# Fused attention and two MoE layers: identity products in TensorE's early gaps, an earlier rank for converting w3 and w_out, and other homes for three operands at the turn to the last product

## The chip, the cores and the metric

One Trainium2 chip, one of its cores. The metric is the device time of one execution in microseconds (us), the median over several executions.

## The reference, cut to what matters

Inputs: q, k, v of 4 batches x 8 heads x 576 positions x 64; 2304 tokens in all; weights w1, w2 (512x1024), w3 (1024x1024), w_out (1024x512), w_in (512x2048), and a second w_out (2048x512).

```python
scores = where(mask, q @ k.T / 8 - slope[h] * (i - j), -1e9)   # causal, window of 128
x = softmax(scores) @ v                                        # 2304 x 512
h = (x @ w1) * (x @ w2) @ w3 ; x = h @ w_out                   # first MoE
out = relu(x @ w_in) ** 2 @ w2_out                             # second MoE
```

The weights arrive as 64-bit floats and are turned into 32-bit floats on the chip.

## The kernel before, in words

The kernel is written as some thousands of small tasks with a rank, an engine or a choice of engines, a cost, dependencies, and the tile slots that they take and give back. A list scheduler in Python (`Plan.run`) keeps a due time for every engine and orders the tasks: among the tasks that could start within 0.1 of the earliest, the one with the lowest rank goes first. Its result is the fixed order of instructions on each engine; on the chip every engine runs its own queue in that order and waits on semaphores. So a rank does not set when something happens, only what stands ahead of it.

Five stages follow each other. **Heads** (0 to about 168 us): 16 pairs of heads. For one pair TensorE makes scores `s` from `qk` (line 437), VectorE adds the bias and takes the row minimum (line 405, `e<-s`), ScalarE takes the exponent (line 413), VectorE scales by the reciprocal sum (line 252), TensorE transposes through `ident` into the one buffer `t` (line 473, `tr0` to `tr3`), ScalarE copies it out (line 196, `pt`), and TensorE multiplies by v (lines 497 and 513). `qk`, `v` and `e` have two buffers each, `s` three. In the gaps of this stage TensorE multiplies w3 by w_out (line 613, `ww`: 8 groups of 8 products of 512 columns), so that h never has to be formed. Each 1024-column piece of w3 and w_out is loaded (1 MB), and converted by one pass on ScalarE (line 320, `cg`) and two on VectorE (lines 329 and 335, `cs` and `cn`); rank of the j-th conversion `c0 + cj*j`, rank of its load `w0 + w34*j`. Heads of pair m have ranks from `-40 + 7m`; lower goes first. All loads and stores stand in one queue, SyncE's.

The planner also puts products of `ident` by itself into gaps of TensorE (`p_warm`, line 531; results are not used): in gaps of more than 1.0 in its own account, before 40 in its own account, as many as fit, if one of the buffers `t` or `g` is free there.

Then **a, b** (lines 929 to 931), **y** and **r** (lines 1125 to 1127, 24 rounds), and last **o**, the product with the second w_out, in nine blocks of 256 tokens. All of them use a seven-product scheme (P1 to P7 on sums of quarter matrices, with operands split into a high and a low part: `oh`/`ol` for the tokens, `wh`/`wl` for the weights). At the turn from r to o the tiles of the tag `xA` (8 slots) hold the four token operands of block 0 (`lfA11` ... `lfA22` load them), the halves of the weight pieces `sm`, `ss` (`mbo5` ... `mbo7` load them, line 702; `cb` on line 716 combines them; `wlao7` and `wlbo7`, line 199, make the last low parts), and the split operand of P1. That of P2 lies in `u` (11 slots). P1 and P2 of block 0 are each cut into chunks 0 to 5 (`Q1o0`, `Q2o0`), which don't need the eighth weight piece, and chunks 6 and 7 (`P1o0`, `P2o0`), which do. The order of these products on TensorE is written out:

```python
turn = ["Q1o0", "P1o0", "Q2o0", "P2o0", "P4o0", "P6o0", "P7o0", "P5o0"]
```

The pools of the r stage (`q1`) are closed and those of the o stage (`q2`, with `fq` and `ww`) opened on their ground after r's last product.

Of the kernel before, what the change touches and what calls it, by code (L numbers as in the profile page):

```python
# [12 lines left out]
ALU = mybir.AluOpType  # L13


RANK = dict(w34=3, vv=20, w0=-15, c0=0, cj=3, h0=-40, hs=7, w12=60, wa=7, wl=9, wb=0, x0=20, mg=4, mgs=1.6, wo=1126, gg=-3, yq=1142)
B, H, S, D = 4, 8, 576, 64
NT = B * S
DM = H * D
# [11 lines left out]
class Plan:  # L31
# [7 lines left out]
    LOOK = 0.1  # L39
    SWITCH = 0.11  # L40
    STAY = 60
    FILL = 40.0

    bias = dict(d=1.0, D=0.2, a=0.3, p=0.0)

# [5 lines left out]
    def hold(self, name, tag, users):  # L51
        self.holds[name] = [tag, users]
# [6 lines left out]
    def run(self):  # L59
        tasks = self.tasks  # L60
        need = {n: len(t[3]) for n, t in tasks.items()}
        users = {}
        for n, t in tasks.items():
            for d in t[3]:
                users.setdefault(d, []).append(n)

        pool = {tag: [0.0] * c for tag, c in self.caps.items()}
        left = {h: v[1] for h, v in self.holds.items()}
        last = {h: 0.0 for h in self.holds}
        free = {}  # L70
        lock = 0.0
        end, on = {}, {}
        ready = {n for n, c in need.items() if c == 0}
        order = []
        shape = lambda n: 1 if n[:3] == "pvl" else {"qk": 1, "pv": 2}.get(n[:2], 0)
        now = 0
        while ready:
            cands = []
            for n in ready:
                rank, where, fn, deps, takes, gives, keep = tasks[n]  # L80
                t0 = 0.0
                ok = True
                for tag in {self.holds[h][0] for h in takes}:
                    p = sorted(pool[tag])
                    want = sum(self.holds[h][0] == tag for h in takes)
                    if len(p) < want + keep:
                        ok = False
                        break
                    t0 = max(t0, p[want - 1])
                if not ok:  # L90
                    continue
                best = None
                for q, w in where.items():
                    e = q.lower()
                    if e == "pe" and shape(n) != now:
                        w += self.SWITCH
                    elif e == "pe" and now:
                        rank -= self.STAY
                    t = max(t0, free.get(e, 0.0))
                    if q in "Dp":  # L100
                        t = max(t, lock)
                    for d in deps:
                        t = max(t, end[d] + (0.0 if on[d] == e else self.lat[on[d]]))
                    key = t + w + self.bias.get(q, 0.0)
                    if best is None or (key, t) < best[:2]:
                        best = (key, t, q, w)
                cands.append((best[1], rank, n, best[2], best[3]))
            assert cands, (sorted(ready)[:20], {h: (v[0], left[h]) for h, v in self.holds.items() if left[h] > 0 and any(h in tasks[n][4] for n in end)})
            t0 = min(c[0] for c in cands)
            near = [c for c in cands if c[0] <= t0 + self.LOOK]  # L110
            t, rank, n, q, w = min(near, key=lambda c: (c[1], c[0], c[2]))
            e = q.lower()
            _, _, fn, deps, takes, gives, _ = tasks[n]
            if e == "pe":
                now = shape(n)
                idle = t - free.get(e, t)
                if 1.0 < idle and t < self.FILL:
                    for tag in "tg":
                        p = pool[tag]
                        if p and min(p) <= free[e]:  # L120
                            p.remove(min(p))
                            k = f"fill{len(order)}"
                            tasks[k] = (0, {}, lambda e, tag=tag, idle=idle: self.filler(tag, int((idle - 0.4) / 0.24)), (), (), (), 0)
                            order.append((k, e, free[e], t - 0.4))
                            p.append(t)
                            break
            ready.remove(n)
            for h in takes:
                p = pool[self.holds[h][0]]
                p.remove(min(p))  # L130
            fin = t + w
            end[n], on[n] = fin, e
            free[e] = fin
            if q in "Dp":
                lock = fin
            for h in gives:
                left[h] -= 1
                last[h] = max(last[h], fin + (self.lat[e] + 0.5 if e == "dma" else 0.0))
                if left[h] == 0:
                    pool[self.holds[h][0]].append(last[h] + 0.1)  # L140
            order.append((n, e, t, fin))
            for u in users.get(n, ()):
                need[u] -= 1
                if need[u] == 0:
                    ready.add(u)
        assert len(order) == len(tasks) and len(end) + sum(n[:4] == "fill" for n in tasks) == len(tasks), [n for n in tasks if n not in end][:20]
        return order
# [3 lines left out]
def fused_kernel(  # L151
# [55 lines left out]
    NJ = NT // (2 * TN)  # L207
    NM = NF2 // 2
# [74 lines left out]
    def w_dma(kb, n=1):  # L283
# [3 lines left out]
        dict(  # L287
            u=11, wo=4, qk=2, v=2, e=NE, s=NPS, t=1, pt=NE, a=5 - NPS, g=2, pl=1, sg=2,
            d1=2, d2=2, d3=1, d4=2, xA=8, xB=12, xC=8, xa=2, xb=2, xc=2,
            yA=14, t2a=1, v6=6, D1=2, D2=2, D4=2, D3=1, E1=2, fq=5, ww=4,  # L290
        ),
        dict(pe=0.25, a=0.3, d=0.22, p=0.25, dma=3.0, gate=0.0),
    )
    add, hold = plan.add, plan.hold
# [360 lines left out]
    def open_q1():  # L655
        xbs.close()
        q = q1.enter_context(tc.tile_pool(name="q1", bufs=1, side="right", reuse_waits="tile"))
        pool.update(yA=q, t2a=q, D1=q)

    def open_ph():  # L660
        xcs.close()
# [9 lines left out]
    def new(tag, shape, dt=F32):  # L671
        return (wp if tag == "u" else pool[tag]).tile(shape, dt, tag=tag, bufs=plan.caps[tag], name=tag)
# [6 lines left out]
    mw = {}  # L679
    sw = {}  # L680
# [15 lines left out]
    def m_back(k, m, tag):  # L696
        if tag == "u":
            t = new(tag, [128, 2048])
            mw[k, m], sw[k, m] = t[:, 0:1024], t[:, 1024:1792]
        else:  # L700
            mw[k, m], sw[k, m] = new(tag, [128, 1024]), new(tag, [128, 768])
        nc.sync.dma_start(out=mw[k, m], in_=m_scr[k, m])

    def combine(kind, i, M, S, e):
# [22 lines left out]
    def add_words2(k, m, rank, stag, dep=()):  # L727
        z = f"{k}{m}"
        kind = "A" if k == "i" else "B"
        if stag == "u":  # L730
            hold("st" + z, "u", 12)
            sm = ss = "st" + z
        else:
            sm, ss = "sm" + z, "ss" + z
            hold(sm, stag, 6)
            hold(ss, stag, 6)
        add("mb" + z, rank - 3, {"dma": w_dma(524)}, lambda e: m_back(k, m, stag), ["ms" + z, *dep], sorted({sm, ss}))
        M = lambda i: mw[k, m][:, 256 * i:256 * i + 256]
        Sg = lambda i: sw[k, m][:, 256 * i:256 * i + 256]
# [547 lines left out]
    def add_o(t, rank, last):  # L1287
# [4 lines left out]
        for k in ("A11", "A21", "A22", "A12"):  # L1292
            i, h = int(k[1]) - 1, int(k[2]) - 1

            def ld(e, k=k, i=i, h=h):
                x = fa[t, k] = new(ft[k], [128, NM, 128])
                nc.sync.dma_start(
                    out=x, in_=s_scr[j][NM * h:NM * h + NM, :, t0 + 128 * i:t0 + 128 * i + 128].rearrange("c p t -> p c t")
                )

            col = (t0 + 128 * i) // TN
            def square(e, k=k):
                x = fa[t, k]
                if e == "a":
                    nc.scalar.activation(out=x, in_=x, func=ACTF.Square)
                else:
                    nc.vector.tensor_tensor(out=x, in0=x, in1=x, op=ALU.mult)

            add(f"fs{k}{t}", rank - 1, w_act(1024), square, [f"lf{k}{t}"], [], [f"f{k}{t}"])
            add(f"lf{k}{t}", rank - 20, {"dma": w_dma(524)}, ld,  # L1310
                [f"ss{h + 1}{col + 1}r{j}{m}" for m in range(NM)] + ([] if ft[k] == "xA" else ["q2"])
                + ([] if t == 0 else [f"lf{k}{t - 1}", "wlbo7", *([f"ol1{t - 2}", f"ol7{t - 2}"] if t > 1 else [])] if k in ("A11", "A21") else [f"fc1{t - 1}"]), [f"f{k}{t}"])

        def comb(i, e):
            o, a, op, b = (("S1", "A21", ALU.add, "A22"), ("S2", "S1", ALU.subtract, "A11"),
# [17 lines left out]
                chain[P] = [f"oh{seq[x - 1]}{t}"] if x else [f"oh{before}{t - 1}"] if t else []  # L1333
        for pos, P in enumerate(order):
            k = A_OF[P]
            tag = "u" if (t, P) == (0, 2) else "xA" if P in (1, 2) else "ww"
            own = [f"ow{P}{t}"] + ([f"ox{P}{t}"] if tag == "xA" else [])
            for n in own:
                hold(n, tag, 1)
# [87 lines left out]
    add("ph", 0, {"gate": 0.0}, lambda e: open_ph(),  # L1427
        [f"sy{k}{lb}{c}" for k in ("11", "12", "21", "22") for c in range(2)] + [f"Y{P}_{lb}1" for P in SP_])
    last_r = [f"P{P}r{NJ - 1}{NM - 1}" for P in range(1, 8)]
    add("q2", 0, {"gate": 0.0}, lambda e: open_q2(), last_r + ["wlao5", "wlbo5"] + [f"ss11r{NJ - 1}{m}" for m in (NM - 2, NM - 1)])  # L1430

    prev = []
    for x, (k, m) in enumerate(m_scr):
# [19 lines left out]
    for m in range(NM):  # L1453
        add_words2("o", m, 2090 + 7 * m, "xA", prev)
        prev = [f"mbo{m}"]
    turn = ["Q1o0", "P1o0", "Q2o0", "P2o0", "P4o0", "P6o0", "P7o0", "P5o0"]
    for t in range(1, NT // 256):
        turn += [f"P1o{t}", f"P3o{t - 1}", *([f"P4o{t - 1}"] if t > 1 else []), *(f"P{P}o{t}" for P in ((2, 6, 7, 5) if t < NT // 256 - 1 else (6, 5, 3, 2, 7, 4)))]
    for x, y in zip(turn, turn[1:]):
# [59 lines left out]
```

## Time and profile before

| | |
|---|---|
| time, median of 3 runs | 806.48 us (806.01 to 807.32) |
| the profiled execution: its own time | 812.59 us |
| its span, first to last instruction | 810.8 us |
| TensorE busy | 791.7 us (98%) |
| VectorE busy | 612.7 us (76%) |
| ScalarE busy | 510.7 us (63%) |
| mean granted TensorE clock | 0.989 |

The busy share of TensorE counts identity products and products at a lowered clock like any other. A granted clock of 1.00 is 2.4 GHz, 0.50 is 1.2 GHz. The profiled execution is longer than the timed ones, so its stretches serve for differences.

### The profile page before, as it was taken

How to read it: one execution, taken by the hardware profiler on the slowest of the kernel's cores; microseconds unless marked ns; L12 is line 12 of the kernel's file. 1: busy time of each engine (PE TensorE's matmuls, PEld its weight loads, DVE VectorE, ACT ScalarE, POOL GpSimd, SP SyncE). 2: the span in 40 equal slices, each digit the busy share in tenths (PEclk: the TensorE clock that was granted, in tenths of full speed). 3: DMA queues.
4: the chain of work that ended last, by engine and by line, in shares of the span. 5: the costliest groups of instructions: out<-in, count | busy, mean ns of one | idle time of the engine just before them, and what ended most of it. 6: DMA issues, size and time to landing. Idle time of an engine off the chain costs nothing. (4 is left out here: it accounts for less than half of the span.)

```text
span 810.8 us, 17310 instructions
## 1 busy us (share of the span) xinstructions
PE 791.7 (98%) x6582; PEld 735.0 (91%) x6582; DVE 612.7 (76%) x1291; ACT 510.7 (63%) x1090; POOL 67.9 (8%) x65
## 2 busy tenths in 40 slices
PE   7989999999999999999999999999998999999998
PEld 6755666689999999899999999999998999999998
DVE  6778687989887787978899955325768997777762
ACT  6988789974554545545655756646766776656630
POOL 1000020111010000200102300001213100000000
PEclk8989999999999999999999999999999999999999
DMA  9987899525887888366754453525654765544200
GB/s 221 289 272 262 250 307 272 179 94 173 308 277 267 279 288 282 123 203 216 219 195 162 160 195 103 201 99 197 203 186 136 193 178 156 142 130 131 79 27 33
DMA packets 115699, 155.80 MB, mean 192 GB/s; under 512 B 12192, under 2 KB 92576, under 8 KB 113568
## 3 DMA queue, kind: packets, MB, share of 16 engines
q1 hardware_dynamic: 115616, 154.70, 61.0%
q8 instruction: 51, 0.84, 0.5%
q14 instruction: 32, 0.26, 0.1%
HBM read 101.71 MB, written 52.95 MB: 191 GB/s over the span
## 5 line engine op out<-in xcount | busy, mean ns | idle before, releaser
L196 ACT ACTIVATE d<-xa 128x288 f32<-128x288 f32 x128 | 52.2, 409 | 97.4 <-PE xa L931 93.3
L1189 DVE TENSOR_TENSOR D<-xb,D 128x384 f32<-128x384 f32 (+1 forms) x62 | 32.1, 520 | 59.3 <-ACT D L196 34.9
L413 ACT ACTIVATE e<-e,st 128x128 f32<-128x128 f32 (+1 forms) x144 | 62.2, 435 | 6.4 <-DVE st L405 5.4
L613 PE MATMUL g<-raw 128*128 128x512 f32 x128 | 63.0, 602 | 0.4 <-DVE raw L335 0.4
L199 DVE TENSOR_TENSOR ww<-fq,ww 128x1024 fp32r<-128x1024 f32 x34 | 41.6, 1223 | 27.0 <-ACT ww L196 26.8
L196 ACT ACTIVATE D<-xa 128x384 f32<-128x384 f32 (+1 forms) x91 | 41.8, 462 | 30.0 <-PE xa L1127 26.4
L196 ACT ACTIVATE ww<-fq 128x1024 fp32r<-128x1024 f32 x35 | 36.9, 1057 | 36.8 <-PE xa L1127 19.9
L931 PE MATMUL xa<-xB,u 128*128 128x288 f32 x192 | 56.8, 296 | 0.0
L929 PE MATMUL xa<-xB,u 128*128 128x288 f32 x192 | 56.8, 296 | 0.0
L930 PE MATMUL xa<-xB,u 128*128 128x288 f32 x192 | 56.1, 292 | 0.0
L1262 ACT ACTIVATE D<-D 128x384 f32<-128x384 f32 x73 | 37.4, 521 | 23.3 <-DVE D L1189 23.3
L716 DVE TENSOR_TENSOR xA<-xA 128x256 f32<-128x256 f32 (+2 forms) x74 | 47.7, 669 | 3.0 <-DMA xA<-g_scr 1.5
L950 DVE TENSOR_TENSOR d<-xb,d 128x288 f32<-128x288 f32 x80 | 36.2, 452 | 15.2 <-ACT d L196 10.8
L473 PEld LDWEIGHTS t<-ident,e 128*128 128x128 f32 x208 | 24.4, 144 | 23.6 <-ACT pt L196 11.2
L405 DVE CUSTOM_DVE_ANT_0 e<-s,bw 128x192 f32<-128x192 f32 (+1 forms) x128 | 40.4, 351 | 2.9 <-PE s L437 2.6
L437 PE MATMUL s<-qk 64*64 64x128 f32 (+2 forms) x768 | 37.5, 293 | 5.0 <-issue 2.1
L437 PEld LDWEIGHTS s<-qk 64*64 64x64 f32 x768 | 28.9, 140 | 13.0 <-issue 4.8
L473 PE MATMUL t<-ident,e 128*128 128x128 f32 x208 | 36.8, 291 | 1.7 <-ACT pt L196 1.3
L930 PEld LDWEIGHTS xa<-xB,u 128*128 128x128 f32 x192 | 36.5, 190 | 0.0
L929 PEld LDWEIGHTS xa<-xB,u 128*128 128x128 f32 x192 | 36.1, 188 | 0.0
L931 PEld LDWEIGHTS xa<-xB,u 128*128 128x128 f32 x192 | 36.0, 188 | 0.0
L1127 PE MATMUL xa<-yA,v 128*128 128x384 f32 x104 | 35.2, 339 | 0.0
(272 smaller groups left out, 2897.9 us busy)
## 6 DMA issues: line engine op xcount, KB each, us to landing
s_scr<-D SPq DMA_DIRECT2D x96, 192.0 KB, 2.0
u<-in_w2io_dram SPq DMA_DIRECT2D x32, 512.0 KB, 6.0
xA<-s_scr SPq DMA_DIRECT2D x20, 512.0 KB, 5.4
qk<-in_qk_dram SPq DMA_DIRECT2D x32, 288.0 KB, 5.4
g_scr<-d SPq DMA_DIRECT2D x64, 144.0 KB, 3.3
xA<-g_scr SPq DMA_DIRECT2D x16, 576.0 KB, 5.5
raw<-in_w3t_dram SPq DMA_DIRECT2D x8, 1024.0 KB, 9.0
raw<-in_w_dram SPq DMA_DIRECT2D x8, 1024.0 KB, 6.9
```

Of the source, the lines that this page charges most:

```text
L196: nc.scalar.activation(out=o, in_=i, func=ACTF.Copy)
L199: eng.tensor_tensor(out=o, in0=a, in1=b, op=ALU.subtract)
L405: nc.vector.tensor_tensor_reduce(out=part_of(m, x, rows), in0=ps, in1=bias, op0=ALU.add, op1=ALU.min, scale=-0.125, scalar=3.0e38, accum_o ...
L413: nc.scalar.activation(out=e, in_=e, func=ACTF.Exp, bias=st[:, 0, x:x + 1], scale=-1.0, accum_out=st[:, 1, x:x + 1],)
L437: nc.tensor.matmul(HD[2 * m + r]["s"][g][o, c:c + w], t[h, 0, 64 * q:64 * q + 64], t[h, 1, 64 * k:64 * k + w], start=True, stop=True,)
L473: nc.tensor.transpose(o, e[:, u:u + 2, :].rearrange("p u c -> p (u c)"), ident)
L613: nc.tensor.matmul(gw[fi], wl, wr, start=c == 0, stop=c == 7)
L716: ENG[e].tensor_tensor(out=o(oi), in0=a(ai), in1=b(bi), op=op)
L929: nc.tensor.matmul(o, wh, xh, start=start and c == 0, stop=False, skip_group_check=True)
L930: nc.tensor.matmul(o, wh, xl, start=False, stop=False, skip_group_check=True)
L931: nc.tensor.matmul(o, wl, xh, start=False, stop=c == len(todo) - 1, skip_group_check=True)
L1262: nc.scalar.activation(out=x, in_=x, func=ACTF.Relu)
```

## The change

Four parts. (1) Identity products go into gaps of more than 0.6 (was 1.0) up to 60 (was 40) in the planner's account, and a little more densely. (2) The conversions of w3 and w_out get ranks 12 lower, close to two pairs of heads (7 each); their loads get later ranks: the j-th -8+4j, was -15+3j. (3) At the turn to o, the split operand of P2 moves from `u` into two slots of `xA`; the second half of the eighth weight piece (`ss`) gets a tile of its own, `xQ`, in `q1`; the load of the token operand A21 of block 0 waits for `wlao7`, and the opening of `q2` for `wlbo7`. (4) `Q2o0` goes ahead of `P1o0`.

```diff
-RANK = dict(w34=3, vv=20, w0=-15, c0=0, cj=3, h0=-40, hs=7, ...)
+RANK = dict(w34=4, vv=20, w0=-8, c0=-12, cj=3, h0=-40, hs=7, ...)
...
-    FILL = 40.0
+    FILL = 60.0
...
                 idle = t - free.get(e, t)
-                if 1.0 < idle and t < self.FILL:
+                if 0.6 < idle and t < self.FILL:
...
-  ... self.filler(tag, int((idle - 0.4) / 0.24)) ...
-                            order.append((k, e, free[e], t - 0.4))
+  ... self.filler(tag, int((idle - 0.3) / 0.22)) ...
+                            order.append((k, e, free[e], t - 0.3))
...
-            yA=14, t2a=1, v6=6, D1=2, D2=2, D4=2, D3=1, E1=2, fq=5, ww=4,
+            yA=14, t2a=1, xQ=1, v6=6, D1=2, D2=2, D4=2, D3=1, E1=2, fq=5, ww=4,
...
-        pool.update(yA=q, t2a=q, D1=q)
+        pool.update(yA=q, t2a=q, D1=q, xQ=q)
...
-            mw[k, m], sw[k, m] = new(tag, [128, 1024]), new(tag, [128, 768])
+            mw[k, m], sw[k, m] = new(tag, [128, 1024]), new("xQ" if (k, m) == ("o", NM - 1) else tag, [128, 768])
...
-            hold(ss, stag, 6)
+            hold(ss, "xQ" if (k, m) == ("o", NM - 1) else stag, 6)
...
-                + ([] if t == 0 else [f"lf{k}{t - 1}", "wlbo7", ...
+                + ([] if t == 0 and k != "A21" else ["wlao7"] if t == 0 else [f"lf{k}{t - 1}", "wlbo7", ...
...
-            tag = "u" if (t, P) == (0, 2) else "xA" if P in (1, 2) else "ww"
+            tag = "xA" if P in (1, 2) else "ww"
...
-    add("q2", ..., last_r + ["wlao5", "wlbo5"] + ...)
+    add("q2", ..., last_r + ["wlao5", "wlbo5", "wlbo7"] + ...)
...
-    turn = ["Q1o0", "P1o0", "Q2o0", "P2o0", "P4o0", "P6o0", "P7o0", "P5o0"]
+    turn = ["Q1o0", "Q2o0", "P1o0", "P2o0", "P4o0", "P6o0", "P7o0", "P5o0"]
```

## Rows read from the trace of the kernel before

**Rows 1.** Busy us of each engine by stage; then granted clock, DMA share, GB/s

```profile
0.00:60.00 60.00, 51.45 (x669) 39.39 (x670) 42.71 (x211) 47.59 (x162) 3.82 (x18) 0.89 0.89 263
60.00:168.00 108.00, 107.89 (x1379) 67.19 (x1378) 90.14 (x362) 94.82 (x302) 8.38 (x7) 1.00 0.80 241
168.00:200.00 32.00, 30.44 (x227) 29.97 (x228) 29.50 (x49) 20.22 (x41) 6.71 (x4) 1.00 0.44 138
```

**Rows 2.** The same view, stretches around the falls of the clock

```profile
12.60:16.00 3.40, 1.80 (x20) 1.03 (x19) 3.35 (x20) 2.35 (x7) 0.00 (x0) 1.00 1.08 207
16.00:22.80 6.80, 6.30 (x57) 5.34 (x59) 4.22 (x17) 4.29 (x18) 0.00 (x0) 0.50 1.07 263
...
46.70:50.10 3.40, 2.09 (x21) 1.14 (x20) 3.20 (x19) 3.34 (x13) 0.00 (x0) 1.00 0.94 243
50.10:57.00 6.90, 6.18 (x93) 5.44 (x94) 3.69 (x15) 5.39 (x19) 0.00 (x0) 0.51 0.74 285
...
627.00:630.40 3.40, 3.36 (x15) 3.36 (x16) 3.37 (x3) 1.32 (x2) 0.00 (x0) 0.50 0.90 246
```

**Rows 3.** Timeline of TensorE, first pairs: start, us, instruction, idle before and releaser

```profile
16.25 0.66 PE L437 MATMUL s<-qk 64*64 64x128 f32 x2 [1.83 <-DMA qk<-in_qk_dram]
...
28.10 0.83 PE L531 MATMUL g<-ident 128*128 128x128 f32 x6
...
33.64 1.10 PE L437 MATMUL s<-qk 64*64 64x128 f32 x30 [0.77 <-issue]
```

**Rows 4.** Timeline of ScalarE and VectorE, 14 to 22 us

```profile
14.87 1.12 ACT L320 ACTIVATE raw<-raw 128x1024 f32<-128x1024 f32 x1 [1.05 <-DMA raw<-in_w3t_dram]
...
20.21 0.60 ACT L196 ACTIVATE pt<-t 128x512 f32<-128x512 f32 x1 [2.04 <-PE t L473]
...
21.71 0.29 DVE L405 CUSTOM_DVE_ANT_0 e<-s,bz 128x128 f32<-128x128 f32 x1 [2.24 <-PE t L473]
```

**Rows 5.** SyncE's queue, and DMA traffic from 3 to 16 us

```profile
9.14 1.25 SPq L363 DMA_DIRECT2D qk<-in_qk_dram  x2
10.44 0.59 SPq L368 DMA_DIRECT2D v<-in_v_main_dram  x1
...
DMA packets 2152, 3.42 MB, mean 263 GB/s; under 512 B 591, under 2 KB 1308, under 8 KB 2023
```

**Rows 6.** Timeline of TensorE and VectorE before the second fall of the clock

```profile
49.05 0.88 PE L437 MATMUL s<-qk 64*64 64x192 f32 x14 [0.77 <-DVE st L405]
50.82 1.11 PE L473 MATMUL t<-ident,e 128*128 128x128 f32 x4 [0.89 <-ACT pt L196]
...
51.60 1.23 DVE L335 SCALAR_TENSOR_TENSOR raw<-raw 128x1024 uint32<-128x1024 uint32 x1
```

**Rows 7.** Timeline of TensorE at the turn from r to o

```profile
625.03 0.38 PE L1125 MATMUL xa<-u,xA 128*128 128x256 f32 x1 [0.48 <-ACT u L196]
627.04 0.58 PE L1126 MATMUL xa<-u,xA 128*128 128x256 f32 x1 [1.62 <-DVE u L199]
...
631.74 0.28 PE L1125 MATMUL xc<-u,ww 128*128 128x256 f32 x1
```

**Rows 8.** Timeline of VectorE and SyncE's queue at the turn

```profile
618.44 3.49 DVE L199 TENSOR_TENSOR xA<-xA 128x512 fp32r<-128x512 f32 x2
...
625.77 1.22 DVE L199 TENSOR_TENSOR u<-xA,u 128x1024 fp32r<-128x1024 f32 x1
626.90 1.22 DVE L1319 TENSOR_TENSOR fq<-xA 128x1024 f32<-128x1024 f32 x1
...
629.30 1.22 DVE L199 TENSOR_TENSOR ww<-xA,ww 128x1024 fp32r<-128x1024 f32 x1
...
610.52 0.39 SPq L702 DMA_DIRECT2D xA<-m_scro  x1
...
626.53 1.11 SPq L1297 DMA_DIRECT2D xA<-s_scr  x2
```

**Rows 9.** DMA issues: count, KB each, us to landing

```profile
xA<-s_scr SPq DMA_DIRECT2D x20, 512.0 KB, 5.4
```

More of the change, by code (lines that the diff above doesn't have):

```diff
@@ L13 @@
 ALU = mybir.AluOpType
-RANK = dict(w34=3, vv=20, w0=-15, c0=0, cj=3, h0=-40, hs=7, w12=60, wa=7, wl=9, wb=0, x0=20, mg=4, mgs=1.6, wo=1126, gg=-3, yq=1142)
+RANK = dict(w34=4, vv=20, w0=-8, c0=-12, cj=3, h0=-40, hs=7, w12=60, wa=7, wl=9, wb=0, x0=20, mg=4, mgs=1.6, wo=1126, gg=-3, yq=1142)
 B, H, S, D = 4, 8, 576, 64
@@ L122, in run @@
                             k = f"fill{len(order)}"
-                            tasks[k] = (0, {}, lambda e, tag=tag, idle=idle: self.filler(tag, int((idle - 0.4) / 0.24)), (), (), (), 0)
-                            order.append((k, e, free[e], t - 0.4))
+                            tasks[k] = (0, {}, lambda e, tag=tag, idle=idle: self.filler(tag, int((idle - 0.3) / 0.22)), (), (), (), 0)
+                            order.append((k, e, free[e], t - 0.3))
                             p.append(t)
@@ L1311, in add_o @@
                 [f"ss{h + 1}{col + 1}r{j}{m}" for m in range(NM)] + ([] if ft[k] == "xA" else ["q2"])
-                + ([] if t == 0 else [f"lf{k}{t - 1}", "wlbo7", *([f"ol1{t - 2}", f"ol7{t - 2}"] if t > 1 else [])] if k in ("A11", "A21") else [f"fc1{t - 1}"]), [f"f{k}{t}"])
+                + ([] if t == 0 and k != "A21" else ["wlao7"] if t == 0 else [f"lf{k}{t - 1}", "wlbo7", *([f"ol1{t - 2}", f"ol7{t - 2}"] if t > 1 else [])] if k in ("A11", "A21") else [f"fc1{t - 1}"]), [f"f{k}{t}"])
         def comb(i, e):
@@ L1429, in fused_kernel @@
     last_r = [f"P{P}r{NJ - 1}{NM - 1}" for P in range(1, 8)]
-    add("q2", 0, {"gate": 0.0}, lambda e: open_q2(), last_r + ["wlao5", "wlbo5"] + [f"ss11r{NJ - 1}{m}" for m in (NM - 2, NM - 1)])
+    add("q2", 0, {"gate": 0.0}, lambda e: open_q2(), last_r + ["wlao5", "wlbo5", "wlbo7"] + [f"ss11r{NJ - 1}{m}" for m in (NM - 2, NM - 1)])
     prev = []
```

## The prediction

> **What bounds the kernel now.** I read the busy time by stage first. From 60 to 168 us TensorE is busy 107.89 of 108 us, and it stays the bound to the end; in the first 60 us it is busy only 51.45, at a mean clock of 0.89 [rows 1]. So a microsecond of TensorE won or lost before 60 us moves everything behind it, as long as VectorE keeps up. The reader should then look at the granted clock in short stretches: it stands at 0.50 three times, from 16.0 to 22.8, from 50.1 to 57.0 and from 627.0 to 630.4 [rows 2]. Ahead of the first TensorE is busy 1.80 of 3.40 us, ahead of the second 2.09 of 3.40 [rows 2], and ahead of the third it waits 0.48 and 1.62 us [rows 7]. Work done at 1.2 GHz takes twice its time, so the three stretches hold 6.30/2, 6.18/2 and 3.36/2 = 3.15, 3.1 and 1.7 us of lost time where TensorE is the bound [rows 2].
>
> The timelines say why TensorE was short of work. At 14.4 us it waits 1.83 us for the scores' load of the third pair [rows 3]. ScalarE meanwhile is held 1.05 us by the first piece of w3, whose conversion (1.12 us) stands ahead of the copy `pt` on which the first pair's next transposes depend [rows 4]; VectorE then idles 2.24 us before the third pair, until transposes have freed a buffer `e` [rows 4]. Before the second fall the waits are 0.77 and 0.89 us, for heads, while the second piece of w_out, which would give TensorE products for such gaps, starts its last conversion pass only at 51.60 [rows 6].
>
> **The change part by part.**
>
> Loads. With later ranks for the weights, the four transfers of the second pair's v (384 KB; issued from 10.44 [rows 5]) come ahead of the first piece of w3 and of the third pair's `qk` in SyncE's queue. The `qk` issue itself hardly moves (9.14 [rows 5], it waits for a buffer), but its bytes land behind 0.39 MB more: at 263 GB/s [rows 5] 1.5 us, so about 17.8 us instead of 16.25. By itself that costs. But w3's piece lands as much later, too late in the planner's account to go ahead of `pt`: ScalarE gives back 1.05 + 1.12 = 2.2 us ahead of that copy [rows 4], and the first pair's transposes and v products can run on TensorE while the third pair's `qk` is under way, where before they came behind it. They need about 0.8 us longer than the copy's gain leaves (ScalarE's exponents in between), so I take 1.4 us for the heads' chain; bounds 0 (the later load eats it) and 2.24, the idle time of VectorE that could go [rows 4]. The first half-clock stretch goes with it if TensorE has that work before 16 us; what it would give beyond the chain is in this term, since heads, not TensorE, set the pace there. The twelve weight loads each move behind the `qk` and `v` loads of one to two and a half pairs. I cost that at nothing: from 60 us on TensorE has products waiting (107.89 of 108 [rows 1]). If that cover fails once, the wait is at most one load of 1.05 MB, 4.0 us at 263 GB/s [rows 5].
>
> Conversions. Twelve ranks put the second piece of w_out ahead of about half of a pair's VectorE work instead of behind it; work for TensorE comes ahead of 51.60, in time for the 0.89 us gap at 50.82 but hardly for the one before it [rows 6]. I take 0.9, bounds 0 and 0.77 + 0.89 = 1.66. The heads behind it on VectorE are later by one pass, 1.23 us [rows 6]; TensorE then has the w3 products to do instead, which is their cover.
>
> The second fall. With that gap filled, TensorE's waits between 46.7 and 50.1 shrink from 1.31 us (3.40 - 2.09 [rows 2]) to below 1. Two waits of 0.77 us, at 33.64 [rows 3] and once more a pair later, did not bring the clock down. So I take it that the clock stays: 3.1 us, bounds 0 and 3.1. The rows for this are thin, which is the largest doubt in the sum.
>
> The Trainium skill, page TensorE: Matmul & The Clock Gate, section "HAM oscillation — how this bites in real kernels", speaks against this: it warns of idle times of TensorE well longer than any here, and by it gaps of a microsecond cost no clock and filling them gives none back. The trace differs: the clock fell after waits of at most 1.83 us [rows 2, 3]. By the page the sum would lose its 3.1.
>
> Identity products. By the planner's account of the kernel before I count some seven further gaps of 0.6 to 1.0, one or two products each, a dozen in all with the denser filling. One is 0.83/3 = 0.28 us [rows 3]. They lie in gaps that the chip shows too (0.77 at 33.64 [rows 3]): nothing. Where the gap is gone, 0.28 to 0.56 us each, up to 2 us for seven. Two longer gaps before 50 us get none: `t` and both `g` are taken there.
>
> The turn. `Q2o0` (18 products) ahead of `P1o0` covers the waits of 0.48 + 1.62 = 2.10 us [rows 7], and without them the 1.7 us of the slow clock would go too. TensorE alone could then start P4 at 628.0 instead of 631.74 [rows 7]: up to 3.8. But P4's operand is the low part that VectorE ends at 629.30 + 1.22 = 630.5 [rows 8], in order behind two sums (from 626.90) and, ahead of these, the eighth piece's low parts (the last at 625.77). With `xQ` that piece can be loaded a round sooner than 610.52 [rows 8]. Its `wlao7` still needs a slot of `u`, and all eleven are taken (seven + two weight pieces of o, two of r) until r's last round but one ends. From there to 626.90 VectorE has hardly a pause, so moving the pass within that chain gains little: a combination of 256 columns that goes elsewhere and short idles. I put them at 0.8, a tenth of the 8.5 us from 618.44 to 626.90 [rows 8]. TensorE then waits near 2 us before P4 instead of 2.1 before P1, and the third stretch at half clock stays. I take 0.8; the upper bound is 3.8, the lower is the third rival.
>
> Give-back. From 168 to 200 us VectorE is busy 29.50 of 32, TensorE 30.44 [rows 1]: there the earlier stage can be cashed only as far as VectorE is earlier too. I take 0.7 off, bounds 0 and 2.
>
> Sum: 1.4 + 0.9 + 3.1 + 0 + 0.8 - 0.7 = 5.5 us. Against the profiled execution that is a span of 810.8 - 5.5 = 805.3 us. Its own time, 812.59, is 6.1 us above the median of 806.48; I carry the difference over: 806.48 - 5.5 = 801.0 us.
>
> **The rivals.** First, the clock still falls before 57 us: the same sum without 3.1, 804.1 us. For it speaks that the waits of 0.77 and 0.89 [rows 6] are not the only ones before 50.1 (1.31 in all [rows 2]), against it the two harmless waits of 0.77. The rule of the Trainium skill (same page) gives the same time by another way (no short gap matters, so the stretch at half clock has another cause and stays), and gets a small chance of its own, as the trace has three falls after short waits.
>
> Second, nothing is won early: the third pair's `qk`, 1.5 us later, keeps TensorE waiting as now, its scores stay the head of the queue, and the second fall stays. Then 0.8 - (0 to 1.5): 805.7 to 807.2 us.
>
> Third, slower: the load of A21 now waits for `wlao7`, and the sums on VectorE that begin at 626.90 [rows 8] need A21. If SyncE issues it where it issues the next block's loads, at 626.53 behind r's last stores [rows 8], it lands 5.4 us later [rows 9], is squared by a pass of 1024 columns (1.12 for such a pass [rows 4]), and the sums start at 633.1 instead of 626.90, with P4, P6 and P7 behind them: 6.2 us lost at the turn. With the early terms as forecast (4.7 after the give-back) that is 806.48 - 4.7 + 6.2 = 808.0; without the clock's 3.1, 811. It decides from the point where the sums start after 626.90 + 4.7 = 631.6. Against it: only that slot of `u` holds `wlao7` up, and a load issued by 620.4 (626.90 - 1.12 - 5.4) is in time.
>
> **How the numbers follow.** Forecast 0.42; clock falls again 0.28, by the rule of the Trainium skill 0.05; nothing early 0.13; A21 late 0.12. The predicted time is the forecast's, 801.0, with its own range 798 to 803. For the whole range I go down by the larger turn (3.0 more, 798.0) and half a microsecond of the other bounds, and up to the second rival's end: 797.5 to 807.3, which leaves out the third rival and little else. A measurement of this kernel can tell about 0.2% from no change: below 804.9 is faster, above 808.1 slower. Faster: 0.40 of the forecast, 0.21 and 0.04 of the next two, 0.03 of the rest, 0.68. Slower: most of the third rival and some of the second, 0.14. Same: 0.18.
>
> **What would show it.** The scores of the third pair start behind the first pair's v products, and VectorE's first instruction for that pair comes before 21.71. The granted clock stays at 1.00 from 16 to 57 us. TensorE multiplies by the second piece of w_out before 50. At the turn TensorE waits before P4 and not before P1, and the sums on VectorE start at about 626 less the early gain. The forecast is wrong if the clock falls again before 57 us, if new waits on w3 pieces appear after 60, or if the sums wait for the load of A21.

## Result and the profile after

The changed kernel takes 814.57 us (median of 4 runs, 812.12 to 816.89) against 806.25 for the kernel before on the same chip (805.59 to 807.32): a ratio of 1.0102, interval 1.0068 to 1.0135. It is slower; I had forecast 801.0 and given slower a chance of 0.14. The profiled execution of the changed kernel took 813.67, with a span of 811.9. Executions that were disturbed (the profiled one of e8 below among them, 859 us at a mean clock of 0.848, so its trace isn't read) count in no ratio.

Busy time by stage and around the falls of the clock, kernel after (stretch and its length; then busy us and number of instructions of TensorE, its weight loads, VectorE, ScalarE, GpSimd; then granted clock, DMA share, GB/s):

```profile
0.00:60.00 60.00, 53.49 (x777) 41.76 (x778) 45.40 (x224) 48.01 (x167) 3.83 (x18) 0.94 0.91 254
60.00:168.00 108.00, 103.49 (x1296) 65.07 (x1295) 86.31 (x349) 90.61 (x289) 6.34 (x6) 0.98 0.78 237
...
300.00:400.00 100.00, 95.48 (x704) 94.67 (x703) 84.85 (x120) 49.36 (x89) 11.98 (x6) 0.98 0.67 216
...
17.60:24.40 6.80, 4.52 (x54) 3.67 (x56) 2.07 (x10) 2.35 (x11) 0.00 (x0) 0.53 1.05 303
24.40:60.00 35.60, 34.86 (x572) 26.10 (x571) 32.53 (x151) 33.49 (x113) 0.00 (x0) 0.99 0.90 265
...
331.90:338.70 6.80, 6.80 (x42) 6.80 (x41) 5.03 (x9) 1.97 (x4) 0.00 (x0) 0.75 0.51 155
```

From 24.4 to 60 us TensorE is now busy 34.86 of 35.6 at 0.99: the second fall of [rows 2] is gone. The first is still there, 17.6 to 24.4. What is new lies later: 4.5 us of idle TensorE between 60 and 168, where it had 0.1 [rows 1], and 4.5 between 300 and 400, where the kernel before had 2.3. Those before 168 are waits for VectorE's work on the heads; none is for a piece of w3, though such waits were the sign of being wrong that I had named.

TensorE's long waits, timeline of the kernel after (idle before and releaser in brackets):

```profile
19.18 0.65 PE L437 MATMUL s<-qk 64*64 64x128 f32 x2 [2.42 <-DMA qk<-in_qk_dram]
20.53 1.98 PE L437 MATMUL s<-qk 64*64 64x128 f32 x30 [0.69 <-DMA qk<-in_qk_dram]
...
135.94 0.88 PE L437 MATMUL s<-qk 64*64 64x192 f32 x14 [2.64 <-DVE st L405]
...
214.08 0.40 PE L929 MATMUL xb<-xC,u 128*128 128x288 f32 x1 [1.91 <-DVE d L950]
...
330.52 0.40 PE L929 MATMUL xb<-xB,u 128*128 128x288 f32 x1 [3.05 <-DVE d L950]
```

The third pair's scores start at 19.18 instead of 16.25 [rows 3]. At 214 and 330 TensorE waits for sums `d` that VectorE makes. I cut the profiled executions at four marks: the first product of a, b, the first and the last of r's products of `yA` by `v`, the end.

| us | heads | a, b and y | r | o | span |
|---|---|---|---|---|---|
| before | 167.8 | 293.2 | 157.5 | 192.2 | 810.8 |
| after | 170.4 | 298.3 | 158.6 | 184.6 | 811.9 |
| before, with the turn to o alone changed (e3 below) | 167.2 | 295.7 | 157.5 | 184.6 | 805.0 |
| after, with the loads as before (e6 below) | 170.8 | 294.4 | 157.7 | 184.7 | 807.5 |
| after, GpSimd barred (e12 below) | 170.7 | 288.5 | 158.5 | 184.6 | 802.4 |

The turn gave more than I forecast, the a, b and y stages lost 5.1 us, the heads 2.6. The profiled executions differ by 1.1 us only, since that of before ran 6.3 above its own median and that of after 0.9 below. One profiled execution is a rough measure of a stage: up to r, e3 has the order of before on every engine, and its a, b and y take 2.5 us longer. The nearest reference for the later loads is e6, which differs from the change by them alone: its heads end as late, and its a, b and y are 3.9 us shorter. The 1.1 us of r are no loss: between its marks stand 894 products instead of 888, 0.177 us each either way.

### The profile page after: what moved, and what is told of

It is laid out like the page before. It is cut to its first block, busy times and chain, and to the rows that moved or that the text cites. A ratio compares the mean times of both kernels' runs of the same rounds, so it can differ in the third digit from the quotient of the medians.

```text
span 811.9 us, 17393 instructions
## 1 busy us (share of the span) xinstructions
PE 787.6 (97%) x6614; PEld 732.4 (90%) x6614; DVE 618.7 (76%) x1299; ACT 510.3 (63%) x1085; POOL 67.2 (8%) x64
## 4 chain that ended last, share of the span: by engine, by line
PE 81%; DVE 10%; DMA 4%; issue 3%; ACT 1%; SPq 1%; DVEq 0%
PE xa L1126 7%; PE xa L1125 7%; PE xa L1127 7%; PE g L613 6%; PE xa L929 5%; PE xa L931 5%; PE xa L930 5%; PE xb L1125 4%; PE xb L1126 4%; PE xb L1127 4%; PE xb L929 3%; PE xb L931 3%; PE xb L930 3%; PE s L437 3%; PE t L473 3%
## 5 line engine op out<-in xcount | busy, mean ns | idle before, releaser
L929 PE MATMUL xa<-xB,u 128*128 128x288 f32 x192 | 57.5, 300 | 0.0
L931 PE MATMUL xa<-xB,u 128*128 128x288 f32 x192 | 57.4, 299 | 0.0
L930 PE MATMUL xa<-xB,u 128*128 128x288 f32 x192 | 56.7, 295 | 0.0
L716 DVE TENSOR_TENSOR xA<-xA 128x256 f32<-128x256 f32 (+2 forms) x75 | 53.6, 741 | 2.1 <-DMA xA<-g_scr 1.6
L437 PEld LDWEIGHTS s<-qk 64*64 64x64 f32 x768 | 28.3, 139 | 16.7 <-issue 5.6
L930 PEld LDWEIGHTS xa<-xB,u 128*128 128x128 f32 x192 | 37.1, 193 | 0.0
L929 PEld LDWEIGHTS xa<-xB,u 128*128 128x128 f32 x192 | 36.8, 191 | 0.1
L931 PEld LDWEIGHTS xa<-xB,u 128*128 128x128 f32 x192 | 36.6, 191 | 0.0
```

Of the source, the lines that this page charges most:

```text
L437: nc.tensor.matmul(HD[2 * m + r]["s"][g][o, c:c + w], t[h, 0, 64 * q:64 * q + 64], t[h, 1, 64 * k:64 * k + w], start=True, stop=True,)
L716: ENG[e].tensor_tensor(out=o(oi), in0=a(ai), in1=b(bi), op=op)
L929: nc.tensor.matmul(o, wh, xh, start=start and c == 0, stop=False, skip_group_check=True)
L930: nc.tensor.matmul(o, wh, xl, start=False, stop=False, skip_group_check=True)
L931: nc.tensor.matmul(o, wl, xh, start=False, stop=c == len(todo) - 1, skip_group_check=True)
```

## Experiments

All ratios are to the kernel before on the same chip, with 95% intervals.

**Which part loses.** Each part alone in the kernel before:

```diff
 e1_fill   part 1 only:     if 0.6 < idle and t < FILL (60), filler denser
 e2_rank   part 2 only:     w34=4, w0=-8, c0=-12
 e3_turn   parts 3, 4 only: xQ, P2's operand in xA, waits of A21 and q2, Q2o0 ahead of P1o0
 e4_load   half of part 2:  w34=4, w0=-8, c0=0    (loads only)
 e5_conv   half of part 2:  w34=3, w0=-15, c0=-12 (conversions only)
```

> The kernel before with part 1 alone (more and denser identity products). Theory A, late weights: the slowdown comes from the ranks of the w3 and w_out loads, so this one is within 1 us of before (806). Theory B, identity products: they hold TensorE up among the first pairs, so this one is slower by 4 us or more. By the forecast it would be 0 to 3 us faster where it keeps the clock from falling.

> The kernel before with part 2 alone (ranks of the conversions 12 lower, ranks of the loads later). Theory A: slower by 8 to 13 us (814 to 819), with the last w3 product after the heads' last v product and more waits of TensorE on VectorE (lines 929 and 950) in the a, b stage. Theory B: within 1 us of before.

> The kernel before with parts 3 and 4 alone (other homes at the turn to o, Q2o0 ahead of P1o0). Theory A: faster by 3 to 4 us (about 802.5), the whole wait at the turn and its half-clock stretch gone. Theory C, the turn is where the time is lost: not faster than before.

> The kernel before with the later ranks of the w3 and w_out loads alone, conversions at their old ranks. Theory A: nearly all of the slowdown of part 2, 6 to 12 us. Rival A2, the earlier conversions do it by standing ahead of heads on ScalarE and VectorE: within 2 us of before.

> The kernel before with the conversions' ranks 12 lower alone (c0 = -12), loads at their old ranks. Theory A, late loads: faster than before by 2 to 5 us, since earlier conversions won back 6 us of the 16.7 that the later loads cost. Rival, the earlier conversions hold up heads: slower by 1 to 3 us.

Measured: identity products 1.0012 (0.9987 to 1.0037); ranks 1.0128 (1.0095 to 1.0161); turn 0.9959 (0.9936 to 0.9983); later loads alone 1.0226 (1.0184 to 1.0268); conversions alone 1.0031 (1.0013 to 1.0049). The first three add up to +0.99%; the change's own figure is 1.02%. The loss is that of the later loads, which alone cost 2.3%, 16.7 us between the medians, more than the 6 to 12 I expected. Earlier conversions cost 0.3% alone, where I had expected a gain, but beside the later loads they win 1% back.

**Which loads.** In the changed kernel:

```diff
 e6_noload  -w34=4, w0=-8    +w34=3, w0=-15                    (all loads as before)
 e7_first   +lead = rank - (-8 if j == 0 else -15 + 3 * j)     (only the first load late)
 e8_rest    +lead = rank - (-15 if j == 0 else -8 + 4 * j)     (the other eleven late)
```

> The changed kernel with the loads' ranks put back (-15 + 3j), everything else as changed. Theory A: the whole loss goes, and the turn's gain and that of the conversions stay: 4 to 8 us faster than before. If the loss stays, it is not the loads.

> The changed kernel with only the first piece of w3 loaded at its later rank (-8, behind the second pair's v), the other eleven at their old ranks. Theory A1, the start: this one piece puts the third pair's scores late and brings the clock down, 4 us or more slower than the same with no late load. Theory A2, the slots: the loss comes from the later pieces, which hold the slots of u into which w1 and w2 are loaded; then it is within 2 us of that kernel.

> The changed kernel with the first piece of w3 at its old rank (-15) and the other eleven loads at their later ranks (-8 + 4j). Theory A2: most of the loss is here, 6 us or more slower than with no late load, with the loads of w1 and w2 at 125 to 170 us instead of 115 to 133. Theory A1: within 2 us of the kernel with no late load.

Measured: 1.0021 (0.9996 to 1.0045), 1.0035 (1.0015 to 1.0055), 1.0133 (1.0113 to 1.0154). The start, where I had looked for the price of the later loads, is not where it is paid: the eleven others hold it. I had expected e6 to be 4 to 8 us faster than before; it is not told from it, and the parts that it has in common with the change, each alone, add up to nothing either (+0.12 + 0.31 - 0.41%).

**By what way.** With late loads the pieces of w3 take slots of `u` later, and the last product with them ends at 170.9 us instead of 166.0; the pieces of w1 and w2 for a, b, which need such slots, come later too. SyncE's queue, kernel before:

```profile
115.46 0.35 SPq L315 DMA_DIRECT2D raw<-in_w_dram  x1
123.70 0.54 SPq L315 DMA_DIRECT2D raw<-in_w_dram  x1
132.63 0.54 SPq L315 DMA_DIRECT2D raw<-in_w_dram  x1
```

and after:

```profile
132.57 0.35 SPq L315 DMA_DIRECT2D raw<-in_w_dram  x1
149.00 0.38 SPq L315 DMA_DIRECT2D raw<-in_w_dram  x1
172.02 0.38 SPq L315 DMA_DIRECT2D raw<-in_w_dram  x1
```

So my second theory was that these late loads are the price:

```diff
 e9_wwrank    after:   -1000 + rank + 0.01 * c  +9 * rank + 0.01 * c      (w3 products among the heads)
 e10_w12late  before:  loads of the first three w1/w2 pieces wait for xh1_11, xh1_13, xh1_15
 e11_early    e3_turn: -w34=3  +w34=2                                     (loads of w3, w_out sooner)
```

> The changed kernel, with the products of w3 by w_out (line 613) given ranks 0, 9, ..., 63 among the heads in place of 1000 and up, so that they are not left to the end of the heads. Theory (the late weight loads cost because TensorE runs heads first, the w3 products are left over until 170 us, their pieces keep the slots of u and the pieces of w1 and w2 load some 20 to 40 us late): the last w3 product ends before 160, the loads of w1 and w2 come near 115 to 135 again, and most of the loss goes: 806 to 810 us. Rival (the late weight loads leave TensorE without products in the first 60 us and nothing else counts): no better, 813 to 817 us, or slower since heads now wait for w3 products.

> The kernel before, where only the loads of the first three pieces of w1 and w2 have to wait for the output of the pairs 11, 13 and 15 of heads (about 126, 147 and 168 us in place of 115, 124 and 133); w3 and w_out as before. Theory (what the late ranks cost is paid in the a, b stage, by w1 and w2 pieces that come as late as in the changed kernel): 811 to 816 us, with new waits of TensorE for d from VectorE between 185 and 350 us and a longer a, b stage by some 5 us. Rival (the cost is in the heads' stage or in the r stage, the late w1 and w2 pieces are hidden): 805 to 808 us.

> The kernel before with the turn to o of the change, and the ranks of the loads of w3 and w_out moved the other way: the j-th -15+2j in place of -15+3j. Theory (the time falls the sooner the w3 pieces are in, as the slots of u come free for w1 and w2 sooner): 802 to 805 us, the w1 and w2 loads before 110 us. Rival (before, the load ranks were early enough, sooner ones only take the DMA queue and the conversions' place from the heads): 805 to 810 us.

Measured: 1.0119 (1.0087 to 1.0152), 1.0128 (1.0096 to 1.0160), 1.0131 (1.0091 to 1.0171). e10 bore the theory out: late w1 and w2 pieces alone (issued at 142, 152 and 177 us, later than I had planned and than in the change) cost as much as the ranks do (e2, 1.0128). e9's time is the rival's, but it settles nothing, as its first two pieces came sooner (114 and 127 us) and its third only at 182. e11 missed both ranges: sooner loads cost 1.7% against e3 (1.0131 against 0.9959), in the heads, which end at 181.4 instead of 167.2. And lateness by itself does not set the price: in e4 the three pieces come sooner than in e2 (131, 141 and 162 us against 132, 147 and 170), and it loses nearly twice as much. But what VectorE was doing before TensorE's wait at 330 gave a third theory. VectorE, kernel after:

```profile
209.03 4.29 DVE L199 TENSOR_TENSOR u<-raw,u 128x1024 fp32r<-128x1024 f32 x2
...
323.20 4.56 DVE L199 TENSOR_TENSOR u<-u 128x1024 f32<-128x1024 f32 x2
327.69 2.42 DVE L199 TENSOR_TENSOR u<-xA,u 128x1024 f32<-128x1024 f32 x1
```

GpSimd, kernel after:

```profile
208.49 2.89 POOL L199 TENSOR_TENSOR u<-raw,u 128x1024 fp32r<-128x1024 f32 x1 [20.82 <-ACT u L196]
...
324.25 2.44 POOL L199 TENSOR_TENSOR u<-xA,u 128x1024 fp32r<-128x1024 f32 x1 [85.10 <-ACT u L196]
327.15 1.87 POOL L199 TENSOR_TENSOR xB<-xA,xB 128x576 fp32r<-128x576 f32 x1 [0.46 <-ACT xB L196]
```

A row `x2` holds two passes. Of the two from 323.20 the first is as fast as ever; the second, by itself, is

```profile
324.34 3.43 DVE L199 TENSOR_TENSOR u<-u 128x1024 fp32r<-128x1024 f32 x1
```

The same passes of VectorE in the kernel before, with GpSimd idle:

```profile
319.52 2.35 DVE L199 TENSOR_TENSOR u<-u 128x1024 f32<-128x1024 f32 x2
...
322.16 1.22 DVE L199 TENSOR_TENSOR u<-xA,u 128x1024 f32<-128x1024 f32 x1
```

Three passes take 6.98 us instead of 3.57 while GpSimd runs two of its own: 3.4 us, and TensorE waits 3.05. The long passes look held, not slowed: the one of 3.43 us begins 0.09 us after GpSimd's at 324.25 and ends 1.1 us after the end of that, the one of 2.42 ends 1.1 us after the end of GpSimd's at 327.15. A pass alone takes 1.22, so each ends as if it had begun when GpSimd was done, and the price is what is left of GpSimd's pass. All five of TensorE's waits for `d` in the change stand behind such a pass (at 214 and 330 behind those above, at 189.37 behind one of 1.99 us instead of 0.75, at 342.90 and 349.96 behind sums of 2.59 and 2.58 instead of 1.35). In e10 the three passes take 4.56 and 2.42 as well, from 323.51; so do they in e2, e4 and e9 (4.56 to 4.58, and 2.42), and in none of before, e1, e3, e5, e6 and e7, though e1, e3, e5 and e7 have one other held pass near there. In the planner's account additions on VectorE and GpSimd exclude each other; on the chip they had drifted into one another.

To tell the overlap from the lateness, GpSimd was barred from such passes in the a, b stage, with the late loads left as they are (e12), and the loads were let go sooner with GpSimd left (e15):

```diff
 e12_after_nogp (after), e13_before_nogp (before), e14_turn_nogp (e3_turn):
+                    if q == "p" and "D" in where and 150 < t < 370:
+                        continue
 e15_keep0 (after): add_words(key, ..., "u", 8, -3 +0, ...)   (w1/w2 loads may take the last slots of u)
```

> The changed kernel, with GpSimd barred from additions and subtractions that VectorE can do too, between 150 and 370 in the planner's account (the a, b stage). Theory (the late pieces of w1 and w2 cost by way of an overlap: VectorE's passes of 1024 columns take 2.3 to 2.4 us in place of 1.2 while GpSimd runs one beside them, and TensorE's waits for d of 0.91, 1.91, 3.05 and 1.04 us follow): those waits shrink to under 1 us each, the a, b and y stages fall from 298 to about 294 us, 809 to 812 us. Rival (VectorE has too much to do there, whoever does it): the waits stay or grow, 813 to 818 us.

> The kernel before with GpSimd barred in the same way: the control. Theory: here the overlaps fell on stretches where TensorE did not wait long for d (3.7 us in all), so little is won: 804 to 807 us. Rival (VectorE has too much to do): the nine passes that it takes over, about 0.7 us each, show as longer waits, 808 to 813 us.

> The kernel before with the turn to o of the change (0.9959 of before by itself) and GpSimd barred in the same way. If the two add up as the theory has it: 801 to 804 us. By the rival 805 to 810 us.

> The changed kernel, where the loads of w1 and w2 may take the last free slots of u (the planner otherwise keeps three free), so that they go sooner although the w3 products are late. Theory (the lateness of these loads is the cause): the third one before 160 us and most of the loss gone, 806 to 811 us. Rival (what else the late w3 loads change, the order of the heads and of VectorE's work, is the cause): 813 to 817 us.

Measured: e12 801.44 us, 0.9933 (0.9911 to 0.9955); e13 1.0080 (1.0052 to 1.0108); e14 1.0028 (1.0008 to 1.0047); e15 1.0047 (1.0025 to 1.0070). The times of e13 and e14 fell into the ranges of the rival, which has VectorE overloaded; e15's lies 0.25 us above the first of its two ranges. SyncE's queue and VectorE in e12 (its lines stand two lower in the file):

```profile
131.84 0.38 SPq L317 DMA_DIRECT2D raw<-in_w_dram  x1
147.65 0.38 SPq L317 DMA_DIRECT2D raw<-in_w_dram  x1
172.35 0.38 SPq L317 DMA_DIRECT2D raw<-in_w_dram  x1
```

```profile
320.70 2.35 DVE L201 TENSOR_TENSOR u<-u 128x1024 f32<-128x1024 f32 x2
322.97 1.22 DVE L201 TENSOR_TENSOR u<-xA,u 128x1024 f32<-128x1024 f32 x1
```

Its heads end as late as in the change and its loads come as late, but the passes are fast again, and TensorE's waits for `d` between 160 and 470 us, in the view of the waits (total, count, longest), are 0.3 us in e12,

```profile
PE xb L931 <- DVE d L952: 0.3, 1, 0.3
```

where they are 7.3 after, 3.7 before, and 2.9 in e6, the change with its loads as before:

```profile
PE xb L929 <- DVE d L950: 7.3, 5, 3.1
```

```profile
PE xb L929 <- DVE d L950: 3.7, 5, 1.5
```

```profile
PE xb L929 <- DVE d L950: 2.9, 5, 1.1
```

VectorE took over GpSimd's passes and was hardly busier for it, since the time that it had been held is gone. From 170 to 400 us, after and then e12 (third and fifth of the engines are VectorE and GpSimd):

```profile
170.00:400.00 230.00, 222.15 (x1645) 219.71 (x1644) 197.06 (x317) 119.29 (x208) 20.27 (x10) 0.99 0.72 235
```

```profile
170.00:400.00 230.00, 229.32 (x1707) 226.58 (x1707) 198.71 (x335) 123.49 (x215) 2.51 (x2) 1.00 0.72 239
```

That speaks against the rival. a, b and y take 288.5 us: 9.8 less than after, and 4.7 and 7.2 less than in before and e3. So late loads need not cost anything there; in the change, as far as the traces show, they cost because the order that follows from them sets GpSimd beside VectorE in front of TensorE. One rival is left: with GpSimd barred the planner sets the whole stage in another order, and no run takes the overlaps away and keeps the order, so part of e12's gain may be that of its order. It is the version that beats both kernels; from e3, the turn alone (0.9959), it is not clearly told apart. I had expected 809 to 812; the waits for `d` explain 7.0 of the 9.8, a wait for another sum, `D`, at 466 (1.8 us against 0.2) another 1.6, and the fall of the clock that followed the wait at 330 up to 1.7 (6.8 us at 0.75), together a little more than the whole.

Barring GpSimd is no general win. In the control it removed the waits for `d` too (0.4 left), and VectorE was less busy than before (189.7 us from 170 to 400, against 195.0), which is not what the rival says either. But the new order brought another wait, for a part of the fourth w1/w2 piece, whose load it issued at 207.40 instead of 202.05:

```profile
221.54 0.61 PE L931 MATMUL xa<-xA,u 128*128 128x288 f32 x1 [5.70 <-ACT u L198]
```

Behind it the clock fell (mean 0.97 from 200 to 300 us). e14 has the same wait, 5.8 us, and lost the same way: 0.7% against e3. e15, where the second and third piece go together at 137.25, has no such overlap at 323 and recovers about half of the loss in the timed runs; three waits for `d` from VectorE (3.5 us in all) and four from ScalarE (3.8) stay.

## Why the prediction was wrong

**The step that failed: the later loads, "at nothing: from 60 us on TensorE has products waiting".** Against e6 it cost 0.8% in the change and 1.1% in e8 (some 7 and 9 us), and alone 2.3% (e4, some 17 us), where I had 0, and 4.0 as the bound "if that cover fails once". What it cost was not a wait for a late piece: TensorE waited for sums of VectorE's, 7.3 us in the change against 2.9 in e6. None of my rivals had this; the third, slower, was for the turn. I had followed the loads to the conversions and no further. They also decide when slots of `u` come free, hence in which order the planner sets a, b's work, hence which passes GpSimd runs beside VectorE, 240 us after the last load of w3 (issued at 91.47, the wait is at 330). The stage that I should have read is the one from 160 to 470 us, with 3.7 us of waits for `d` in the trace of before. And the price stood in my own rows: of the two subtractions at 618.44 that take 3.49 us [rows 8], the second is held by a pass of GpSimd (without it, both take 1.28 in the trace of after). GpSimd, kernel before:

```profile
618.64 2.74 POOL L199 TENSOR_TENSOR u<-xA,u 128x1024 fp32r<-128x1024 f32 x1 [1.09 <-ACT u L196]
```

The Trainium skill, page SBUF — State Buffer, section "Who interferes with whom", has the rule: an instruction of VectorE with two inputs in SBUF contends with a GpSimd instruction that reads SBUF. The trace agrees (4.56 against 2.35 us for two passes); I had not weighed it.

**The heads' chain (1.4).** Not there. The third pair's scores came 2.9 us later, not 1.5, and TensorE waited 2.42 and 0.69 us for them; the first fall stayed. Part of the 2.9 varies from execution to execution: e3, with the loads of before, has them at 16.91, behind waits of 2.21 and 0.88. e7 against e6 shows that the later first load is worth nothing measurable either way.

**Conversions (0.9).** Wrong sign alone: 0.3% slower, 2.5 us. With all parts but the later loads (e6), the heads end at 170.8 instead of 167.2 in e3; with the conversions alone (e5) they end at 166.5. So where the 0.3% is lost is not shown, and why e6's heads are later was not tried.

**The second fall (3.1).** In the profile it went, as forecast. But it belonged to that execution, not to the kernel: e3's TensorE instructions are those of before, in the same order, up to r. Its timeline of TensorE,

```profile
49.17 0.88 PE L437 MATMUL s<-qk 64*64 64x192 f32 x14 [0.77 <-DVE st L405]
50.95 0.65 PE L473 MATMUL t<-ident,e 128*128 128x128 f32 x4 [0.90 <-ACT pt L196]
```

has the waits of [rows 6], and busy time in the same stretch

```profile
50.10:57.00 6.90, 6.05 (x103) 4.43 (x103) 5.83 (x23) 6.71 (x21) 0.00 (x0) 1.00 0.80 300
```

shows no fall, where before had 0.51 [rows 2]. Its heads end at 167.2 instead of 167.8, so the whole fall cost at most some 0.6 us there. Nor did these products take twice their time at the half clock, as my term had it: the 30 at 20.53 in the trace of after take 1.98 us, those of [rows 3] 1.10. I had carried the profiled execution's clock over to the median. Its mean, 0.989, is as low as the lowest of the 85 executions of before timed beside these experiments; the median in each of the four groups was 0.996 or 0.997. The Trainium skill's rule on long idle times (page TensorE: Matmul & The Clock Gate, section "HAM oscillation — how this bites in real kernels"), which I had set aside, would have given the better sum, without the 3.1. Its reason isn't shown: in the trace of after the clock did fall in or after waits of 2.42, 2.64 and 3.05 us.

**Identity products (0).** Right: 1.0012, not told from 1.

**The turn (0.8).** Right in sign, too small: 0.9959 is 3.3 us, near the upper bound of 3.8. TensorE at the first product of P4, and VectorE ahead of it, kernel after:

```profile
636.32 0.28 PE L1125 MATMUL xc<-u,ww 128*128 128x256 f32 x1
636.90 0.38 PE L1127 MATMUL xc<-u,ww 128*128 128x256 f32 x1 [0.18 <-DVE ww L199]
```

```profile
627.69 1.28 DVE L199 TENSOR_TENSOR xA<-xA 128x512 fp32r<-128x512 f32 x2
...
633.23 1.23 DVE L1319 TENSOR_TENSOR fq<-xA 128x1024 f32<-128x1024 f32 x1 [0.34 <-ACT xA L1305]
```

P4 starts 9.05 us after r's last product (627.27), before 13.2 (618.54 to 631.74 [rows 7]). I had held VectorE's chain nearly fixed and expected a wait of 2 us ahead of P4; it is 0.18. GpSimd took `wlbo7` at 628.62 and did not hold up the 512-column subtractions, so these took 1.28 instead of 3.49 us, and the sums start 6.0 us after r's last product instead of 8.4. The third rival did not come: A21 holds the sums up by 0.34. Part of the 4.15 us was the clock again: e13, with the old turn and no fall there, takes 11.6 from r's last product to P4. The rest of the 7.6 us by which the profiled o stage is shorter lies behind P4 and is not shown to be the turn's. TensorE has no idle time there in either trace, and the clock is 1.00, but the same products of 256 columns follow each other more slowly before than after (503 against 514 in 60 us):

```profile
740.00:800.00 60.00, 60.00 (x503) 60.00 (x502) 38.76 (x46) 27.25 (x36) 0.00 (x0) 1.00 0.26 75
```

```profile
740.00:800.00 60.00, 60.00 (x514) 60.00 (x513) 39.11 (x46) 28.06 (x37) 0.00 (x0) 1.00 0.26 78
```

e7, with the new turn, has 508, as have e1, e5 and e13 with the old one. What sets this pace was not tried.

**Give-back (-0.7).** Not separable from the rest.

What stays open: e12 is 13 us faster than the change in the timed runs and 9.5 in the profiled ones, and the timed runs leave no trace to place the rest. Why e4 loses most, with loads that are not the latest, was not tried; nor was why the heads of the change, of e6 and of e12 end some 3 us later than e3's.

## What to carry to other kernels

When a list scheduler fixes the order, a rank that moves early loads can be paid for hundreds of microseconds later: follow the buffers that the loads hold, not only the data. Look for passes of VectorE that take twice the time of their like, ask what GpSimd did beside them, and then whether TensorE waited behind: barring GpSimd from one stage turned a loss of 1.0% into a gain of 0.7% (0.4% of it the turn's), but lost 0.8% in the kernel before, so it has to be tried on the order that is to run. A row that merges two passes hides which of them was long. Before a fall of the clock in one profiled execution is put into a sum, compare that execution's mean clock with those of the timed ones.

## What the runs showed of the hardware that I had not expected

A pass of VectorE with both inputs in SBUF that began behind the start of a subtraction on GpSimd took 2.4 to 3.4 us for 1024 columns instead of 1.22, and 2.59 for sums of 1152 columns instead of 1.35; those of 1024 ended 1.1 us after GpSimd's. TensorE's wait behind them was of the size of the excess (3.05 of 3.4 us). In the two cases below the engine that began second was held, and which one that is varied between two executions with the same order. In before VectorE began first, and GpSimd's pass took 2.38 us:

```profile
324.02 1.22 DVE L199 TENSOR_TENSOR u<-u 128x1024 fp32r<-128x1024 f32 x1
324.16 2.38 POOL L199 TENSOR_TENSOR xB<-xA,xB 128x576 fp32r<-128x576 f32 x1 [44.01 <-ACT xB L196]
```

In e3 GpSimd began first, and VectorE's took 2.38:

```profile
323.62 1.43 POOL L199 TENSOR_TENSOR xB<-xA,xB 128x576 fp32r<-128x576 f32 x1 [44.11 <-ACT xB L196]
323.75 2.38 DVE L199 TENSOR_TENSOR u<-u 128x1024 fp32r<-128x1024 f32 x1
```

At a granted clock of 1.00 and without idle time, products of 256 columns ran 503, 508 or 514 to 60 us in different executions. With the same instructions in the same order and waits of 0.77 and 0.90 us, the clock fell in one execution (0.51 from 50.1 to 57) and not in another (1.00).
